# Issuing the store of a block's four sums from GpSimd in stage up 1

## The chip, the cores and the metric

One core of a Trainium2 chip. The metric is device time in microseconds, the median of several runs. Engines are named TensorE (PE in the profile; PEld are its weight loads), VectorE (DVE), ScalarE (ACT), GpSimd (POOL) and SyncE (SP). A "q" behind a name (SPq) is that engine's instruction queue.

## The reference, cut to what matters

Random-feature attention, then two feed-forward layers, all in float32:

```
x = favor_attention(q, k, v, omega)            # (2304, 512)
h = x @ w_in;   x = (h * sigmoid(h)) @ w_out   # 512 -> 2048 -> 512: up 1, down 1
g = x @ w_gate; v = x @ w_val                  # 512 -> 1536: up 2
out = (silu(g) * v) @ w_out2                   # 1536 -> 512: down 2
```

The weights of the feed-forward layers come to the kernel as 64-bit floats.

## The kernel before, in words

The program is one stream per engine, written out in advance. Its stages follow one another: attention, up 1, down 1, up 2, down 2. Each product of up and down is split into seven half-size products (a Strassen-like scheme), so a weight block is needed not only as its four quarters A11, A12, A21, A22 but also in four sums S1 to S4. Operands are split into a high and a low part, and each product is three matmuls.

**Converting a weight block** (`conv_job`, L339 on). Two loads bring the raw 64-bit words of the halves (L344). ScalarE takes the upper word (`first`, L368), VectorE shifts it (L375) and merges the lower word (`low`, L382), after which the raw slot is free again. Then GpSimd makes S1 to S4 (`sums`, L401) into one buffer of 1024 columns, which in up 1 exists once (`f_sum`). What follows depends on the block:

- a block of `w_in` is used in up 1 itself: it is split into high and low parts (`hi`, L433 on VectorE and L435 on ScalarE; `lo`, L448), and the buffer of sums is free after the last split;
- a block of moe_w_out (`down_job`) or the first block of gate and val (`up_job_dram`) is needed later: three stores put it into DRAM (L465): A22 (128 KB), A11 and A12 (256 KB), and the four sums (512 KB). The buffer of sums is free when the last has landed.

During attention three blocks of each kind are converted (there the list `early` is worked off). In up 1 the stream `conv` does the rest: blocks 3 to 7 of `w_in` and of moe_w_out by turns, then gate and val (`conv1`, at the end of the function).

**Up 1** (`up_phase(0, ...)`). For each of 24 steps seven products run on TensorE (L1133). ScalarE copies a partial result from one PSUM bank to the next or to SBUF (L1150), VectorE adds another (L1207), ScalarE applies SiLU (L1174), and SyncE stores the result (L1159).

**What sets the order.** A planner in the kernel's own Python keeps a clock per engine (`clk`), a price per kind of operation (`cost`, `dma_cost`) and a due time per result (`T`). Before each product `flush` writes out, in order of planned time, what the streams have ready. Of each stream and engine only the first entry may be placed (of the `conv` stream's ScalarE list the first two). An operation on a list can't pass the one ahead of it, and on the chip each engine works through its instructions in the order written. A DMA is an operation of its issuing engine: the planner books 0.35 us of SyncE for its issue, then a start, a duration by size and a lag, after which it counts as landed. All loads and stores of up 1 are issued by SyncE.

Of the kernel before, what the change touches and what calls it, by code (L numbers as in the profile page):

```python
# [11 lines left out]
U32 = mybir.dt.uint32  # L12
# [30 lines left out]
def kernel(  # L43
# [13 lines left out]
    nc = tc.nc  # L57
    ctx.enter_context(tc.manual_schedule())
    P = 128
# [3 lines left out]
    S = 576  # L63
# [16 lines left out]
    FP = (w_in.shape[0], w_gate.shape[0])  # L80
    wsrc = {"in": w_in, "out": w_out, "gate": w_gate, "val": w_val, "out2": w_out2}
    wsrc = {k: w.bitcast(U32) for k, w in wsrc.items()}
# [6 lines left out]
    wd_d = {k: tc.dram_tile([7, P, FP[m] * 256], F32, name=f"wd_{k}") for m, k in enumerate(DNK)}  # L89
    wu_d = {k: tc.dram_tile([P, 7 * 256], F32, name=f"wu_{k}") for k in UPK[1]}  # L90
# [12 lines left out]
    def cut(t, o, n):  # L103
        return t[:, o : o + n]
# [39 lines left out]
    clk = {e: 0.0 for e in ("PE", "ACT", "DVE", "POOL", "SP", "dma", "slot", "landed")}  # L144
# [3 lines left out]
    def cost(kind, n):  # L148
        a, b = fixed[kind]
        return a + b * n  # L150

    class Op:
        __slots__ = ("eng", "cost", "fn", "ins", "outs", "guard", "then", "slots", "live", "lead")

# [20 lines left out]
        def emit(self):  # L175
            t = max(clk[self.eng], self.ready())
            clk["slot"] = 0.0
            if self.eng == "SP":
                took, lag = self.cost
                clk["SP"] = t + 0.35  # L180
                clk["dma"] = max(t + 1.55, clk["dma"]) + took
                clk["end"] = clk["landed"] = clk["dma"] + lag
            else:
                clk["end"] = t + self.cost
            self.fn()
            if self.eng == "SP":
                end = clk["landed"]
            else:
                clk[self.eng] = end = t + self.cost
            for k in self.outs:  # L190
                T[k] = end
            if self.then is not None:
                self.then(end)
# [3 lines left out]
    def dma_cost(nbytes, kind="rows"):  # L197
        a, b = RATE[kind]
        return nbytes * a, b
# [125 lines left out]
    f_raw = Free("raw", [cut(fa, R_AT + i * 1024, 1024) for i in range(2)])  # L325
# [8 lines left out]

    halved = []

    def conv_job(kind, i, dram=None, side=False):
        b = {}
        key = lambda *k: (kind, i, *k)  # L339

        def load(h):
            def go():
                b["r", h] = r = f_raw.take()
                nc.sync.dma_start(out=r.bitcast(U32), in_=wsrc[kind][i, h])  # L344

            def then(end):

                if kind != "out2":
                    T[key("r", h)] = end + (1 if kind in ("in", "out") else 2.5)
                else:  # L350
                    T[key("r", h)] = end + 6.0

            return Op("SP", dma_cost(P * 4096, "words"), go, outs=[key("r", h)], slots=(f_raw, 1), then=then)

        def word(h, w):
            return b["r", h].bitcast(U32).rearrange("p (c w) -> p c w", w=2)[:, :, w]
# [32 lines left out]
        def blk(n):  # L389
            if n in ("A21", "A22"):  # L390
                return cut(b["c", 0], 0 if n == "A21" else 256, 256)
            if n in ("A11", "A12"):
                return cut(b["c", 1], 0 if n == "A11" else 256, 256)
            return cut(b["S"], 256 * (int(n[1]) - 1), 256)

        def sums(n, l, r, ins):
            def go():
                if n == 1:
                    b["S"] = f_sum.take()
                f = nc.gpsimd.tensor_add if n == 1 else nc.gpsimd.tensor_sub  # L400
                f(blk(f"S{n}"), blk(l), blk(r))  # L401

            return Op(
                "POOL", cost("POOL", 256), go, ins=[key(*k) for k in ins], outs=[key("S", n)],
                slots=(f_sum, 1) if n == 1 else None,
            )


        parts = ((0, 1), (1, 3), (3, 5), (5, 7))
        after = ([("f", 0)], [("f", 1)], [("S", 1), ("S", 2)], [("S", 3), ("S", 4)])  # L410

        def src(k):
            if k == 0:
                return blk("A22")
            return b["c", 1] if k == 1 else cut(b["S"], 512 * (k - 2), 512)

        def done(t):
            f_c.give(b["c", 0], t)
            f_c.give(b["c", 1], t)
            f_sum.give(b["S"], t)  # L420
# [34 lines left out]
            eng = "POOL" if side else "DVE"  # L455
            return Op(eng, cost(eng, n), go, ins=[key("hi", k)], outs=outs)

        def store(a, z, src, ins):

            b["stores"] = 3  # L460

            def go():
                o = dram(a, z)
                t = src()
                nc.sync.dma_start(out=o, in_=t.rearrange("p (o c) -> p o c", c=256) if len(o.shape) == 3 else t)  # L465
                b["stores"] -= 1
                if not b["stores"]:
                    done(clk["landed"])

            return Op("SP", dma_cost(P * (z - a) * 1024, "parts"), go, ins=[key(*x) for x in ins], outs=[key("d", a)])  # L470

        half = [load(0), load(1), first(0), first(1), shift(0), low(0), shift(1), low(1)]
        if dram is not None:
            return [
                *half,
                sums(1, "A21", "A22", [("f", 0)]),
                sums(3, "A11", "A21", [("f", 0), ("f", 1)]),
                store(0, 1, lambda: blk("A22"), [("f", 0)]),
                store(1, 3, lambda: b["c", 1], [("f", 1)]),
                sums(2, "S1", "A11", [("f", 1)]),  # L480
                sums(4, "A12", "S2", [("f", 1)]),
                store(3, 7, lambda: b["S"], [("S", n) for n in range(1, 5)]),
            ]
        f0, f1 = ("f", 0), ("f", 1)
        return [
# [25 lines left out]
    def weave(*jobs):  # L511

        ops = [*jobs[0][:8]]
        for n, j in enumerate(jobs):
            new = deque(jobs[n + 1][:8] if n + 1 < len(jobs) else ())
            for _ in range(min(2, len(new))):
                ops.append(new.popleft())
            for i, o in enumerate(j[8:]):
                ops.append(o)
                if i % 2 and new:  # L520
                    ops.append(new.popleft())
            ops += new
        return ops

    def down_job(m, i):
        k = DNK[m]
        return conv_job(
            k, i, dram=lambda a, z: wd_d[k][a:z, :, i * 256 : (i + 1) * 256].rearrange("o p c -> p o c")
        )

    def up_job_dram(k):
        return conv_job(k, 0, dram=lambda a, z: wu_d[k][:, a * 256 : z * 256])

    early = {"conv": deque(), "x": deque()}

# [184 lines left out]
    def u_of(u, b):  # L720
        return u // UB, UB * (u % UB) + b
# [185 lines left out]
    def store(u):  # L907
        B, p = u_of(u, 0)
        for b in range(UB):
            T["xd", B, p + b] = 0.0  # L910
            made["xd", B, p + b] = (step_of[0], 3, "out")
        nc.sync.dma_start(
            out=x_d[B][p : p + UB].rearrange("b p s -> p b s"), in_=xts.pop(u).rearrange("p (b s) -> p b s", b=UB)
        )
# [5 lines left out]
    for t in spare_c:  # L920
        f_c.give(t, 0.0)
    f_sum.give(spare_sum, 0.0)
    early["conv"].extend(chain(*(conv_job("in", i, side=True) for i in range(3)), *(down_job(0, i) for i in range(3))))
    early["x"].extend(x_prep(0, 0, xr1, False, "POOL", early=True))
    def two_steps(d):
# [78 lines left out]
    first_up = conv_job("in", 3)  # L1004
    for x in first_up[:2]:
        x.emit()
    for f, some in ((f_c, spare_c), (f_sum, [spare_sum])):
        n = len(f.q)
# [588 lines left out]
        lambda: x_prep(0, 2, xr2, False, "DVE", before=1, then=xr2_end),  # L1597
    ]

    rest = deque(down_job(0, i) for i in range(3, FP[0]))  # L1600
    jobs = []
    for i in range(3, FP[0]):
        jobs += [conv_job("in", i) if i > 3 else first_up, rest.popleft()]
    jobs += rest
    jobs += [up_job_dram("gate"), up_job_dram("val")]
    conv1 = [x for x in weave(*jobs) if not any(x is y for y in first_up[:2])]
    opened = []
    extra_c, extra_raw = cut(fa, XR_AT, 512), cut(fa, XR_AT + 512, 1024)
# [108 lines left out]
    jobs = []  # L1717
    for i in range(1, FP[1]):
        jobs += [conv_job("gate", i), conv_job("val", i), down_job(1, i - 1)]
# [75 lines left out]
```

## Time and profile before

| | us |
|---|---|
| median of three runs | 827.8 (827.64 to 830.42) |
| the profiled execution | 828.38 |
| its span, first to last instruction | 826.6 |
| TensorE busy in it | 814.5 |
| VectorE, ScalarE, GpSimd busy | 615.1, 558.5, 162.4 |

The profile is of one execution. A row of a timeline gives start, duration, engine, source line, operation, output and input; in brackets stands how long the engine was idle before it and what ended that. Up 1 runs from about 118 to 290 us of the span, down 1 to about 482, up 2 to about 692. TensorE has its full clock in all of it.

### The profile page before, as it was taken

To read this page: it belongs to the slowest core of one execution; us is meant where nothing else is said; L and a number is where in the kernel's file an instruction comes from. 1 tells how busy PE (TensorE), PEld (TensorE's weight loads), DVE (VectorE), ACT (ScalarE), POOL (GpSimd) and SP (SyncE) were. 2 spreads that over 40 slices of the span, in tenths; PEclk is the share of its full clock that TensorE was granted. 3 is DMA by queue.
4 is the path that set the end of the run, shared out by engine and by line. 5 is a ranking of instruction groups with operands and counts; after the bars stand their busy time and mean duration, and the time that the engine had idled before them with its cause. 6 is when DMAs were issued, how large, how long until landed. Compare 5 with 4: busy or idle time off the path is not lost.

```text
span 826.6 us, 18058 instructions
## 1 busy us (share of the span) xinstructions
PE 814.5 (99%) x6889; PEld 794.8 (96%) x6889; DVE 615.1 (74%) x982; ACT 558.5 (68%) x1172; POOL 162.4 (20%) x204
## 2 busy tenths in 40 slices
PE   8999999999999999999999999999999999999998
PEld 7878889999999999999999999999999999999998
DVE  4888877657744598995989987675656559998872
ACT  6989978867767776455577776665656558655552
POOL 0477851033442000000000113130303020000000
PEclk9999999999999999999999999999999999999999
DMA  8679956679889996538366836463636278764502
GB/s 281 197 249 277 315 186 218 201 223 328 288 266 374 395 306 213 170 115 267 116 212 230 271 102 211 126 213 105 212 107 216 101 235 318 250 217 140 164 3 77
DMA packets 112134, 175.58 MB, mean 212 GB/s; under 512 B 9648, under 2 KB 94256, under 8 KB 112048
## 3 DMA queue, kind: packets, MB, share of 16 engines
q1 hardware_dynamic: 111824, 174.20, 63.7%
q8 instruction: 54, 0.88, 0.4%
q10 hardware_dynamic: 224, 0.23, 0.1%
q14 instruction: 32, 0.26, 0.1%
HBM read 109.38 MB, written 65.01 MB: 211 GB/s over the span
## 4 chain that ended last, share of the span: by engine, by line
PE 81%; issue 6%; ACT 4%; DMA 4%; DVE 2%; POOL 1%; SPq 1%; ACTq 0%; DVEq 0%; POOLq 0%
PE ps L1133 36%; PE ps L1556 35%; PE ps L777 3%; ACT kq L793 2%; PE ps L821 2%; PE ps L837 2%; PE ps L868 2%; DMA fa<-in_moe_w_out 1%; POOL fa L401 1%; DMA g_d<-fa 1%; DMA ra<-wd_out 1%; PE ps L893 1%; DMA rawq<-in_q 1%; DVE fa L382 1%; ACT qp L839 1%
## 5 line engine op out<-in xcount | busy, mean ns | idle before, releaser
L401 POOL TENSOR_TENSOR fa<-fa 128x256 f32<-128x256 f32 x124 | 103.4, 848 | 496.2 <-DMA x_d<-fa 202.9
L1133 PE MATMUL ps<-ra 128*128 128x384 f32 x840 | 143.0, 327 | 2.2 <-ACT ps L1150 2.2
L1133 PE MATMUL ps<-rb,ra 128*128 128x384 f32 x840 | 142.4, 327 | 0.8 <-ACT ps L1150 0.8
L1133 PE MATMUL ps<-rc,ra 128*128 128x384 f32 x840 | 141.1, 326 | 0.0
L1133 PEld LDWEIGHTS ps<-ra 128*128 128x128 f32 x840 | 137.1, 189 | 3.5 <-ACT ps L1150 3.5
L1133 PEld LDWEIGHTS ps<-rb,ra 128*128 128x128 f32 x840 | 137.2, 189 | 2.0 <-ACT ps L1150 1.9
L1133 PEld LDWEIGHTS ps<-rc,ra 128*128 128x128 f32 x840 | 137.2, 189 | 0.0
L1150 ACT ACTIVATE ps<-ps 128x384 f32<-128x384 f32 x180 | 85.8, 478 | 67.2 <-PE ps L1133 58.1
L1367 ACT ACTIVATE ra<-fa 128x768 fp32r<-128x768 f32 x81 | 68.0, 843 | 64.2 <-PE ps L1556 55.1
L1556 PE MATMUL ps<-ra,rb 128*128 128x384 f32 x576 | 96.5, 326 | 0.0
L1556 PEld LDWEIGHTS ps<-ra,rb 128*128 128x128 f32 x576 | 94.1, 189 | 0.0
L1371 DVE TENSOR_TENSOR ra<-fa,ra 128x768 fp32r<-128x768 f32 x80 | 76.2, 954 | 19.6 <-ACT ra L1367 18.9
L793 ACT ACTIVATE kq<-ps,nb 128x128 f32<-128x128 f32 x288 | 79.4, 408 | 6.2 <-DVE nb L791 6.1
L1207 DVE TENSOR_TENSOR fa<-fa,ps 128x384 f32<-128x384 f32 x78 | 43.0, 552 | 35.7 <-ACT ps L1150 26.2
L1556 PE MATMUL ps<-ra 128*128 128x384 f32 x414 | 69.2, 326 | 0.0
L1556 PE MATMUL ps<-ra,rc 128*128 128x384 f32 x402 | 68.8, 326 | 0.0
L1556 PEld LDWEIGHTS ps<-ra 128*128 128x128 f32 x414 | 67.6, 189 | 0.0
L1556 PEld LDWEIGHTS ps<-ra,rc 128*128 128x128 f32 x402 | 65.9, 189 | 0.0
L1391 DVE TENSOR_TENSOR fa<-ra,fa 128x768 f32<-128x768 f32 x63 | 60.1, 954 | 0.9 <-DMA ra<-g_d 0.4
L382 DVE SCALAR_TENSOR_TENSOR fa<-fa 128x512 uint32<-128x512 uint32 x65 | 58.7, 903 | 0.7
L368 ACT ACTIVATE fa<-fa 128x512 f32<-128x512 f32 x65 | 54.3, 838 | 4.4 <-DMA fa<-in_moe_w_out 2.7
L791 DVE TENSOR_REDUCE nb<-ps 128x4 f32<-128x512 f32 x72 | 48.4, 682 | 6.3 <-PE ps L777 3.2
(128 smaller groups left out, 1153.2 us busy)
## 6 DMA issues: line engine op xcount, KB each, us to landing
g_d<-fa SPq DMA_DIRECT2D x110, 192.0 KB, 3.8
fa<-g_d SPq DMA_DIRECT2D x42, 384.0 KB, 4.6
ra<-g_d SPq DMA_DIRECT2D x42, 384.0 KB, 4.0
fa<-in_moe_w_out SPq DMA_DIRECT2D x28, 512.0 KB, 5.2
g_d<-mf SPq DMA_DIRECT2D x58, 192.0 KB, 3.9
fa<-in_moe_w_in SPq DMA_DIRECT2D x16, 512.0 KB, 5.2
wd_out<-fa SPq DMA_DIRECT2D x12, 512.0 KB, 3.3
fa<-in_moe_w_gate SPq DMA_DIRECT2D x12, 512.0 KB, 4.1
```

Of the source, the lines that this page charges most:

```text
L368: nc.scalar.activation(c, word(h, 1).bitcast(F32), AF.Prelu, scale=2.0**-112, alpha=-(2.0**32))
L382: nc.vector.scalar_tensor_tensor(c, word(h, 0), 29, c, op0=ALU.logical_shift_right, op1=ALU.bitwise_or)
L401: f(blk(f"S{n}"), blk(l), blk(r))
L791: nc.vector.reduce_max(nb, x, axis=AX.X, negate=True)
L793: nc.scalar.activation(e[:, g // 2, g % 2, h * M : (h + 1) * M], x[:, g, :], AF.Exp, bias=nb[:, g : g + 1])
L1133: nc.tensor.matmul(woven(ps[b][:, :N]), cut(l, j * P, P), halves(cut(r, j * N, N)), start=start and c == 0, stop=stop and c == 5, skip_gro ...
L1150: nc.scalar.activation(out() if callable(out) else out, src, AF.Copy)
L1207: nc.vector.tensor_add(t, t if in_place else p5[n], ps[bank_][:, :N])
L1367: nc.scalar.activation(ops[s, p, k][0], src(), AF.Copy)
L1371: nc.vector.tensor_sub(l, src(), h.bitcast(F32))
L1391: (nc.gpsimd if eng == "POOL" else nc.vector).tensor_sub(z(PLACE[to]), z(PLACE.get(l, l)), z(PLACE.get(r, r)))
L1556: nc.tensor.matmul(woven(ps[BANKS[p] + e][:, :N]), cut(a, e * P, P), halves(b), start=p in FIRST and i == 0 and c == 0, stop=p in LAST and ...
```

## The change

The store of the four sums gets an engine of its own choice: with "S" in the new argument `own` it is an operation of GpSimd, issued with `nc.gpsimd.dma_start`, in the list of GpSimd behind the sums. The planner books 1.0 us of GpSimd for the issue, and the same start, duration and lag as for SyncE. The blocks of up 1 get `own="S"`; those of attention and of up 2 keep the default. The same argument could move loads ("L"), which no block asks for.

```
+    ISSUE = {"SP": 0.35, "POOL": 1.0}
...
-            if self.eng == "SP":
+            if isinstance(self.cost, tuple):
                 took, lag = self.cost
-                clk["SP"] = t + 0.35
+                clk[self.eng] = t + ISSUE[self.eng]
                 clk["dma"] = max(t + 1.55, clk["dma"]) + took
                 clk["end"] = clk["landed"] = clk["dma"] + lag
...
-        def store(a, z, src, ins):
+        def store(a, z, src, ins, eng="SP"):
...
-                nc.sync.dma_start(out=o, in_=t.rearrange("p (o c) -> p o c", c=256) if len(o.shape) == 3 else t)
+                by = nc.gpsimd if eng == "POOL" else nc.sync
+                by.dma_start(out=o, in_=t.rearrange("p (o c) -> p o c", c=256) if len(o.shape) == 3 else t)
...
-            return Op("SP", dma_cost(P * (z - a) * 1024, "parts"), go, ins=[key(*x) for x in ins], outs=[key("d", a)])
+            return Op(eng, dma_cost(P * (z - a) * 1024, "parts"), go, ins=[key(*x) for x in ins], outs=[key("d", a)])
...
-                store(3, 7, lambda: b["S"], [("S", n) for n in range(1, 5)]),
+                store(3, 7, lambda: b["S"], [("S", n) for n in range(1, 5)], "POOL" if "S" in own else "SP"),
...
-    rest = deque(down_job(0, i) for i in range(3, FP[0]))
+    OWN = "S"
+    rest = deque(down_job(0, i, OWN) for i in range(3, FP[0]))
...
-    jobs += [up_job_dram("gate"), up_job_dram("val")]
+    jobs += [up_job_dram("gate", OWN), up_job_dram("val", OWN)]
```

## Rows read from the trace of the kernel before

**Rows 1.** The page, part 1: busy us, share of the span, instructions.
```profile
PE 814.5 (99%) x6889; PEld 794.8 (96%) x6889; DVE 615.1 (74%) x982; ACT 558.5 (68%) x1172; POOL 162.4 (20%) x204
```

**Rows 2.** Windows: start:end, us, busy us (instructions) by engine, clock, DMA share, GB/s.
```profile
118.00:290.00 172.00, 169.49 (x1072) 166.91 (x1072) 110.83 (x196) 129.22 (x268) 42.88 (x48) 1.00 0.85 289
482.00:692.00 210.00, 210.00 (x1294) 210.00 (x1294) 136.16 (x234) 130.25 (x263) 47.96 (x60) 1.00 0.53 177
692.00:827.00 135.00, 131.06 (x807) 130.76 (x805) 103.38 (x124) 73.85 (x112) 0.00 (x0) 1.00 0.46 152
```

**Rows 3.** Waits of the weight loads, 115 to 292 us; then their timeline.
```profile
PEld ps L1133 <- ACT ps L1150: 4.7, 8, 1.5
...
190.35 0.95 PEld L1133 LDWEIGHTS ps<-ra 128*128 128x128 f32 x6 [0.53 <-ACT ps L1150]
...
195.01 0.95 PEld L1133 LDWEIGHTS ps<-rb,ra 128*128 128x128 f32 x6 [0.79 <-ACT ps L1150]
...
233.52 0.95 PEld L1133 LDWEIGHTS ps<-ra 128*128 128x128 f32 x6 [1.48 <-ACT ps L1150]
235.04 10.70 PEld L1133 LDWEIGHTS ps<-ra 128*128 128x128 f32 x66 [0.58 <-ACT ps L1150]
```

**Rows 4.** SyncE's queue: its waits, 170 to 262 us; then its timeline.
```profile
SPq L465 <- POOL fa L401: 12.3, 6, 3.2
...
179.31 0.50 SPq L344 DMA_DIRECT2D fa<-in_moe_w_out  x1
181.44 0.45 SPq L344 DMA_DIRECT2D fa<-in_moe_w_in  x1
...
222.00 3.94 SPq L465 DMA_DIRECT2D wd_out<-fa  x2
225.99 0.50 SPq L344 DMA_DIRECT2D fa<-in_moe_w_out  x1
```

**Rows 5.** Timeline of GpSimd in up 1.
```profile
182.23 2.93 POOL L401 TENSOR_TENSOR fa<-fa 128x256 f32<-128x256 f32 x4 [3.37 <-DMA wd_out<-fa]
196.80 2.93 POOL L401 TENSOR_TENSOR fa<-fa 128x256 f32<-128x256 f32 x4 [3.39 <-DMA wd_out<-fa]
212.43 2.92 POOL L401 TENSOR_TENSOR fa<-fa 128x256 f32<-128x256 f32 x4 [3.40 <-DMA wd_out<-fa]
220.74 4.80 POOL L401 TENSOR_TENSOR fa<-fa 128x256 f32<-128x256 f32 x4 [5.39 <-DVE ra L448]
229.64 2.91 POOL L401 TENSOR_TENSOR fa<-fa 128x256 f32<-128x256 f32 x4 [4.10 <-DMA wd_out<-fa]
```

**Rows 6.** Timeline of VectorE in up 1.
```profile
174.50 0.76 DVE L382 SCALAR_TENSOR_TENSOR fa<-fa 128x512 uint32<-128x512 uint32 x1
...
191.66 1.19 DVE L382 SCALAR_TENSOR_TENSOR fa<-fa 128x512 uint32<-128x512 uint32 x1
...
221.18 0.79 DVE L382 SCALAR_TENSOR_TENSOR fa<-fa 128x512 uint32<-128x512 uint32 x1
```

**Rows 7.** Timeline of ScalarE in up 1.
```profile
185.87 0.62 ACT L435 ACTIVATE ra<-fa 128x512 fp32r<-128x512 f32 x1
...
189.06 0.86 ACT L368 ACTIVATE fa<-fa 128x512 f32<-128x512 f32 x1 [0.65 <-DMA fa<-in_moe_w_in]
...
193.34 0.53 ACT L1174 ACTIVATE fa<-fa 128x384 f32<-128x384 f32 x1 [1.18 <-DVE fa L1207]
...
201.10 0.61 ACT L435 ACTIVATE ra<-fa 128x512 fp32r<-128x512 f32 x1
...
216.61 0.62 ACT L435 ACTIVATE ra<-fa 128x512 fp32r<-128x512 f32 x1
...
232.42 0.66 ACT L368 ACTIVATE fa<-fa 128x512 f32<-128x512 f32 x1 [2.49 <-DMA fa<-in_moe_w_out]
...
236.79 0.61 ACT L435 ACTIVATE ra<-fa 128x512 fp32r<-128x512 f32 x1
```

**Rows 8.** All transfers that write or read wd_out: issue to landing.
```profile
DMA to landing us min/median/max: 1.9/5.0/7.9
```

More of the change, by code (lines that the diff above doesn't have):

```diff
@@ L185, in emit @@
             self.fn()
-            if self.eng == "SP":
+            if isinstance(self.cost, tuple):
                 end = clk["landed"]
@@ L335, with conv_job @@
     halved = []
-    def conv_job(kind, i, dram=None, side=False):
+    def conv_job(kind, i, dram=None, side=False, own=""):
         b = {}
@@ L343, in go @@
                 b["r", h] = r = f_raw.take()
-                nc.sync.dma_start(out=r.bitcast(U32), in_=wsrc[kind][i, h])
+                (nc.gpsimd if "L" in own else nc.sync).dma_start(out=r.bitcast(U32), in_=wsrc[kind][i, h])
             def then(end):
@@ L351, in then @@
                     T[key("r", h)] = end + 6.0
-            return Op("SP", dma_cost(P * 4096, "words"), go, outs=[key("r", h)], slots=(f_raw, 1), then=then)
+            return Op("POOL" if "L" in own else "SP", dma_cost(P * 4096, "words"), go, outs=[key("r", h)], slots=(f_raw, 1), then=then)
         def word(h, w):
@@ L523, in weave, with down_job, up_job_dram @@
         return ops
-    def down_job(m, i):
+    def down_job(m, i, own=""):
         k = DNK[m]
         return conv_job(
-            k, i, dram=lambda a, z: wd_d[k][a:z, :, i * 256 : (i + 1) * 256].rearrange("o p c -> p o c")
+            k, i, dram=lambda a, z: wd_d[k][a:z, :, i * 256 : (i + 1) * 256].rearrange("o p c -> p o c"), own=own
         )
-    def up_job_dram(k):
-        return conv_job(k, 0, dram=lambda a, z: wu_d[k][:, a * 256 : z * 256])
+    def up_job_dram(k, own=""):
+        return conv_job(k, 0, dram=lambda a, z: wu_d[k][:, a * 256 : z * 256], own=own)
     early = {"conv": deque(), "x": deque()}
@@ L1598 @@
     ]
-    rest = deque(down_job(0, i) for i in range(3, FP[0]))
+    OWN = "S"
+    rest = deque(down_job(0, i, OWN) for i in range(3, FP[0]))
     jobs = []
     for i in range(3, FP[0]):
-        jobs += [conv_job("in", i) if i > 3 else first_up, rest.popleft()]
+        jobs += [conv_job("in", i, own=OWN) if i > 3 else first_up, rest.popleft()]
     jobs += rest
-    jobs += [up_job_dram("gate"), up_job_dram("val")]
+    jobs += [up_job_dram("gate", OWN), up_job_dram("val", OWN)]
     conv1 = [x for x in weave(*jobs) if not any(x is y for y in first_up[:2])]
```

## The prediction

> **What bounds the kernel now.** I read the page's table of engines first: TensorE has work for 99% of the span [rows 1]. Then the stages, each as one window: up 1 has 169.49 us of matmul in 172.00 us, up 2 has none to spare (210.00 in 210.00), and what is missing in down 2 (131.06 in 135.00) is mostly the end of the program [rows 2]. The change touches up 1, so its own matmul sets the limit and all that an edit can give back is what TensorE waits there. The waits of the weight loads say how much that is: 4.7 us in 8 waits, every one for a ScalarE copy of L1150 [rows 3]. Four of them carry most: 0.53 and 0.79 us near 190 and 195 us, 1.48 and 0.58 us near 233 and 235 us [rows 3].
>
> Next, why ScalarE was late with those copies. It works in order. At 232.42 it had stood 2.49 us in front of a conversion (L368) whose raw weights had not landed; the copy that TensorE wanted was behind it. At 189.06 the same with 0.65 us [rows 7]. And why had the weights not landed? SyncE's queue is in order too. The two stores that begin at 222.00 take until 225.94, because the second is the store of the four sums and stands until GpSimd has made them (220.74 + 4.80 = 225.54); the load of moe_w_out is issued at 225.99, right behind it [rows 4, 5]. The raw slot that this load fills had been free since the VectorE operation that began at 221.18 ended, at 221.97 [rows 6]. So the load stood 4 us behind a store that it has nothing to do with. The queue's waits give the sum for all of them: SyncE stood 12.3 us in 6 waits for GpSimd's sums [rows 4].
>
> **The change part by part.** Seven stores of 512 KB leave SyncE's queue: five blocks of moe_w_out (indices 3 to 7) and the single blocks of gate and val. The three blocks converted during attention don't get the new argument, and up 2's don't either. Loads stay where they are, because the argument holds no "L".
>
> *Removed from SyncE:* seven issues (about 0.4 us each, under other work and worth nothing by themselves) and the 12.3 us of standing. In the planner the store also leaves SyncE's list of the conversion stream, of which only the first entry may be placed, so the next loads are planned earlier as well as run earlier. At 222 us: the load goes at about 222.4 in place of 225.99, 3.6 us sooner. With the 6.4 us that it then took to release ScalarE (225.99 to 232.42), it has landed by 228.8; ScalarE was free for it from 229.93 (232.42 - 2.49). The wait goes, and with it 1.48 + 0.58 = 2.06 us of TensorE. At 179.31 the first load follows a store of sums in the same way, and the load of 181.44, the third in that train, is what ScalarE stood for at 189.06 [rows 4, 7]; the train starts some 3 us sooner, so this 0.53 us goes too. The 0.79 us at 195.01 I don't count: there ScalarE stood 1.18 us for VectorE, not for a load [rows 7]. Gain: 2.06 + 0.53 = 2.6 us. What is late next at those places is PE's own rate.
>
> *Added to GpSimd:* seven issues, between a block's four sums and the next block's four. No row shows a transfer issued by GpSimd, so neither the issue nor the landing has a price. GpSimd's own time costs nothing: behind the store it stands anyway until the one buffer of sums is free, 3.39 us and 4.10 us in the rows [rows 5]. What counts is by how much the next sums are later than now; call it L. Queued behind them are the next `w_in` block's sums, and ScalarE's conversion of S3 and S4 (L435, 128x512) waits for these. The slack between the last sum and that conversion, over the four blocks: 185.16 to 185.87 = 0.71; 199.73 to 201.10 = 1.37; 215.35 to 216.61 = 1.26; 232.55 to 236.79 = 4.24, of which 2.06 goes with the stall, so 2.18 [rows 5, 7]. TensorE gives another 0.4 us (2.49 us of ScalarE cost 2.06). A block thus costs nothing until L passes 1.1, 1.8, 1.7 and 2.6 us. Bounds for L: transfers of this tensor land 1.9 to 7.9 us after issue, median 5.0 [rows 8]; against the 3.4 to 4.1 us that the store of sums needs now, L lies between -2.2 and 4.5. At the low end nothing is lost. I take the median, 5.0 - 3.4 = 1.6 and 5.0 - 4.1 = 0.9, and round up to L = 1.5: the store now starts on a queue that has drained while SyncE stood, and will run beside loads issued ahead of it. That costs 1.5 - 1.1 = 0.4 us in the first block and nothing in the others.
>
> The Trainium skill names a hazard here: by "SBUF — State Buffer", section "SBUF: two separate sides", a transfer issued by GpSimd has its descriptors written by GpSimd's cores, and VectorE in a two-port mode locks them out until its instruction ends. No run here shows such a transfer yet; by the page's figures (620 ns alone, 3,100 ns beside a VectorE copy) L would be about 2.5 us, an estimate, and the change would come out even. This hazard is the mechanism of the slower rival below, where its price is worked out from rows.
>
> *VectorE beside GpSimd:* the same operation (L382) takes 0.76 and 0.79 us mostly alone and 1.19 us at 191.66, beside sums [rows 6]. A store may hold up one VectorE operation as the sums do, by 0.4 us; bounds 0 (VectorE has room in up 1) and 7 x 0.4 = 2.8 us. Nearer is the low end, since the trace shows one such delay among its waits of TensorE (at 195.01): I take 0.6.
>
> *Moved elsewhere:* SyncE's later loads of down 1 start when the conversion stream is empty; they sit 20 us ahead of need, and the last store now leaves when its sums end. I take 0, bounds ±1 us for how ScalarE's order falls there.
>
> **Sum.** -2.6 + 0.4 + 0.6 = -1.6 us, all of it in up 1. The profiled execution took 828.38 us (span 826.6 and 1.8 around it); it would be 826.8. The median of the runs, 827.8, lies 0.6 lower, and becomes 826.2.
>
> **The rivals.**
> *No change* (827.8, within 0.7): the stall moves rather than goes. The seven loads start sooner, and a store on its own queue takes bandwidth from them; ScalarE meets the next late operand instead, and 195.01 shows that VectorE stands ready to be that. Against it: at 233 us nothing else was late within 2 us. The Trainium skill speaks for this rival: "DMA: Bandwidth & Descriptors", section "Issuing engines are not separate DMA queues", says that issuing from several engines saves only issue time; by that rule the gain is seven issues under other work, and the time stays 827.8. The trace disagrees as to what that saves here, since SyncE stood 12.3 us in order, not in issue.
>
> *Slower, by late sums.* One mechanism: the store issued by GpSimd lands so late that ScalarE stands in front of S3 and S4 of the `w_in` blocks, as it does now in front of raw weights. Gain and loss cancel at L = 2.4 (1.3 + 0.6 + 0.7 + 0 = 2.6). At L = 3.5 it costs 2.4 + 1.7 + 1.8 + 0.9 = 6.8, net +4.2: 832.0. At the bound, 4.5: 3.4 + 2.7 + 2.8 + 1.9 = 10.8, net +8.2: 836.0. For it: the first block's slack is only 0.71 us, and the planner prices the landing as for SyncE. Against: the median landing leaves L at 1.5.
>
> *All stalls go:* the planner's new order happens to remove every wait of up 1; -4.3 us (4.7 less what the matmul pipe hides): 823.5. The waits after 260 us have other causes, so little speaks for it.
>
> **How the numbers follow.** About 0.5% (4.1 us) is what a measurement of this kernel tells from no change. Forecast 0.54 (its own range 824.6 to 827.2), no change 0.23, slower 0.20, all stalls 0.03. More than 0.5% faster needs nearly every stall of up 1: 0.03. More than 0.5% slower needs L above 3.5, about half of the slower case, and something for an unlucky new order: 0.13. The rest, 0.84, is within. The range 824.0 to 832.0 leaves out the last case and the far end of the third.
>
> **What would show it.** Right: no wait of SyncE for GpSimd's sums in up 1; loads of moe_w_out issued some 3 us sooner against the sums; ScalarE's 2.49 us in front of L368 gone; TensorE's waits in up 1 down from 4.7 to 2 to 3 us; down 1 starting 1 to 2 us sooner. Wrong: ScalarE waiting for GpSimd at L435, or GpSimd standing 6 us and more for its store; a row of VectorE operations stretched at the seven issues; new waits in up 2, whose order I take to be as before.

## The result, and the profile after

The change makes the kernel slower by 1.1%: 835.66 us in the median of 6 runs, against 827.72 us for the kernel before in the same comparison. The ratio is 1.0108, with a 95% interval of 1.009 to 1.0127. The forecast was 826.2 us, the range 824.0 to 832.0. What came is the rival "slower, by late sums". Of the ten times of one kernel below (two buffers, the change) one was 1710.22 us, at the full clock and for a reason that is not known; its ratio leaves that one out.

Up 1 is where it is lost. Its first product starts at 117.2 us of the span (118.4 before, with nothing changed ahead of it), and down 1's first product at 295.6 (289.6 before): up 1 takes 178.4 us in place of 171.2. After it the two executions differ by 0.5 us.

First, the wait that the change was to remove. SyncE's timeline after, at the block of [rows 4]'s line at 179.31: the loads of moe_w_out go out at 174.52, three microseconds before the sums of the block ahead are made (172.87 + 4.78 = 177.65).

```profile
174.10 0.37 SPq L468 DMA_DIRECT2D wd_out<-fa  x1
174.52 2.05 SPq L346 DMA_DIRECT2D fa<-in_moe_w_out  x2
```

SyncE no longer waits for GpSimd's sums between 170 and 262 us. Nor does ScalarE stand for raw weights to speak of: 0.6 us in one wait, where it stood 2.49 and 0.65 us [rows 7]. Of the waits of TensorE at 190, 195, 233 and 235 us [rows 3] the last three have gone with it; at 190 the same weight loads wait longer than before (191.08 below), for another reason.

Now what has come in. GpSimd's timeline after, beside [rows 5]; L468 is the store that it now issues, the bracket what it waited for:

```profile
172.87 4.78 POOL L403 TENSOR_TENSOR fa<-fa 128x256 f32<-128x256 f32 x4 [42.08 <-DVE ra L450]
177.95 1.12 POOL L468 DMA_DIRECT2D wd_out<-fa  x1 [0.31 <-POOL fa L403]
185.04 4.18 POOL L403 TENSOR_TENSOR fa<-fa 128x256 f32<-128x256 f32 x4 [5.98 <-DMA wd_out<-fa]
...
209.87 5.56 POOL L403 TENSOR_TENSOR fa<-fa 128x256 f32<-128x256 f32 x4 [3.73 <-DVE ra L450]
215.73 0.77 POOL L468 DMA_DIRECT2D wd_out<-fa  x1 [0.30 <-POOL fa L403]
222.95 3.85 POOL L403 TENSOR_TENSOR fa<-fa 128x256 f32<-128x256 f32 x4 [6.46 <-DMA wd_out<-fa]
```

The last sum of a block ends at 177.65 and the next block's first begins at 185.04: 7.4 us, where the kernel before needed 3.4. At 215.43 to 222.95 it is 7.5 us. So L, the lateness that the prediction put at 1.5 us, is 4.0. The sums themselves also ran longer: 4.18, 3.11, 3.85 and 3.43 us for the four `w_in` blocks, where the kernel before needed 2.91 to 2.93. Counted from the last sum of the block ahead, the last sum of these four blocks thus comes 5.3, 4.1, 5.1 and 3.7 us later than before. ScalarE's waits (total, times, longest) and its timeline show who pays:

```profile
ACT ra L437 <- POOL fa L403: 10.0, 3, 4.2
```

```profile
184.54 0.49 ACT L1153 ACTIVATE ps<-ps 128x384 f32<-128x384 f32 x1
189.26 0.63 ACT L437 ACTIVATE ra<-fa 128x512 fp32r<-128x512 f32 x1 [4.23 <-POOL fa L403]
189.79 0.47 ACT L1153 ACTIVATE fa<-ps 128x384 f32<-128x384 f32 x1
...
226.84 0.63 ACT L437 ACTIVATE ra<-fa 128x512 fp32r<-128x512 f32 x1 [3.84 <-POOL fa L403]
...
243.36 0.63 ACT L437 ACTIVATE ra<-fa 128x512 fp32r<-128x512 f32 x1 [1.91 <-POOL fa L403]
```

It stands in front of the conversion of S3 and S4, and the copy that TensorE needs (L1153) is written behind it. TensorE's waits over up 1, and the large ones:

```profile
PEld ps L1136 <- ACT ps L1153: 10.1, 7, 3.7
```

```profile
191.08 0.95 PEld L1136 LDWEIGHTS ps<-ra 128*128 128x128 f32 x6 [2.60 <-ACT ps L1153]
...
227.90 0.95 PEld L1136 LDWEIGHTS ps<-rc,ra 128*128 128x128 f32 x6 [3.73 <-ACT ps L1153]
...
247.88 2.90 PEld L1136 LDWEIGHTS ps<-ra 128*128 128x128 f32 x18 [2.13 <-ACT ps L1153]
```

The first two, 2.60 and 3.73 us, follow ScalarE's two long stands. The third has another cause: the copy that ends it stood behind an operation (L1177) that waited for an addition of VectorE.

```profile
246.38 0.52 ACT L1177 ACTIVATE fa<-fa 128x384 f32<-128x384 f32 x1 [1.62 <-DVE fa L1210]
...
247.36 0.47 ACT L1153 ACTIVATE ps<-ps 128x384 f32<-128x384 f32 x1
```

The same 18 weight loads wait 1.87 us in a kernel below in which ScalarE never stands for sums.

10.1 us in place of 4.7 is 5.4 of the 7.2 us. Another 1.7 is a slower clock after the first of these waits: 24 weight loads from 192.00 took 5.61 us, where 24 at the full clock take 3.93.

```profile
192.00 5.61 PEld L1136 LDWEIGHTS ps<-rb,ra 128*128 128x128 f32 x24
...
200.50 3.93 PEld L1136 LDWEIGHTS ps<-rc,ra 128*128 128x128 f32 x24
```

The windows below (PE, PEld, DVE, ACT and POOL busy with instructions, then the granted clock) give the same: a clock of 0.53 and of 0.62 for 2 us each loses 0.94 + 0.76 = 1.7 us.

```profile
190.00:192.00 2.00, 0.92 (x6) 0.92 (x6) 1.05 (x3) 2.00 (x5) 0.72 (x1) 1.00 0.52 189
192.00:194.00 2.00, 2.00 (x8) 2.00 (x8) 1.97 (x4) 1.00 (x3) 1.04 (x2) 0.53 0.15 51
194.00:196.00 2.00, 2.00 (x10) 2.00 (x9) 1.10 (x2) 1.55 (x4) 1.62 (x2) 0.62 0.98 192
196.00:198.00 2.00, 2.00 (x14) 2.00 (x13) 1.65 (x3) 0.97 (x2) 0.78 (x1) 1.00 1.06 372
```

### The profile page after: what moved, and what is told of

Same layout as the page of the kernel before. It is cut to its first block, busy times and chain, and to the rows that moved or that the text cites. A ratio compares the mean times of both kernels' runs of the same rounds, so it can differ in the third digit from the quotient of the medians.

```text
span 833.0 us, 18059 instructions
## 1 busy us (share of the span) xinstructions
PE 817.0 (98%) x6889; PEld 797.2 (96%) x6889; DVE 620.8 (75%) x982; ACT 557.3 (67%) x1172; POOL 172.1 (21%) x211
## 4 chain that ended last, share of the span: by engine, by line
PE 79%; issue 6%; DMA 5%; DVE 3%; POOL 3%; ACT 3%; SPq 1%; ACTq 0%; POOLq 0%; DVEq 0%
PE ps L1559 34%; PE ps L1136 34%; PE ps L780 4%; POOL fa L403 3%; DMA wd_out<-fa 2%; PE ps L824 2%; PE ps L840 2%; PE ps L871 2%; ACT kq L796 1%; DMA g_d<-fa 1%; DVE fa L384 1%; PE ps L896 1%; DMA rawq<-in_q 1%; DVE ra L450 0%; ACT fa L370 0%
## 5 line engine op out<-in xcount | busy, mean ns | idle before, releaser
L403 POOL TENSOR_TENSOR fa<-fa 128x256 f32<-128x256 f32 x124 | 107.2, 878 | 490.4 <-ACT fa L1177 222.5
L1136 PEld LDWEIGHTS ps<-rb,ra 128*128 128x128 f32 x840 | 138.9, 191 | 0.3 <-ACT ps L1153 0.3
L1153 ACT ACTIVATE ps<-ps 128x384 f32<-128x384 f32 x180 | 85.6, 476 | 71.0 <-PE ps L1136 64.2
L1210 DVE TENSOR_TENSOR fa<-fa,ps 128x384 f32<-128x384 f32 x76 | 41.9, 551 | 33.8 <-ACT ps L1153 24.8
L384 DVE SCALAR_TENSOR_TENSOR fa<-fa 128x512 uint32<-128x512 uint32 x65 | 61.0, 939 | 0.7
```

Of the source, the lines that this page charges most:

```text
L384: nc.vector.scalar_tensor_tensor(c, word(h, 0), 29, c, op0=ALU.logical_shift_right, op1=ALU.bitwise_or)
L1136: nc.tensor.matmul(woven(ps[b][:, :N]), cut(l, j * P, P), halves(cut(r, j * N, N)), start=start and c == 0, stop=stop and c == 5, skip_gro ...
L1153: nc.scalar.activation(out() if callable(out) else out, src, AF.Copy)
L1210: nc.vector.tensor_add(t, t if in_place else p5[n], ps[bank_][:, :N])
```

## The experiments

Two things changed at once: who issues the store, and the planner's order (the loads pass the store in its lists). And one thing had to be explained: why the store takes 7.4 us to give its buffer back. In the table, "gap" is the time from the last sum of a moe_w_out block to the next block's first where the landing ended the wait, and "stands" is ScalarE's wait for sums. Blocks are compared in up 1 unless said otherwise.

| kernel | median us | ratio to before (95%) | gap us | stands us |
|---|---|---|---|---|
| before | 827.4 to 827.9 | | 3.4 to 4.1 | 0 |
| the change | 835.66 | 1.0108 (1.009 to 1.0127) | 6.8 to 7.5 | 10.0 |
| new order, SyncE issues | 830.42 | 1.0043 (1.0025 to 1.0061) | 4.4 to 7.4 | 5.7 |
| old order, GpSimd issues | 841.0 | 1.0172 (1.0147 to 1.0196) | 6.4 to 9.2 | 14.8 |
| the change, planner told | 839.72 | 1.0143 (1.0128 to 1.0158) | 6.6 to 7.6 | 4.9 |
| gate and val only | 828.4 | 1.0009 (0.9996 to 1.0022) | | 0 |
| two buffers, the change | 828.09 | 1.0006 (0.9996 to 1.0016) | | 0 |
| two buffers, before | 827.49 | 0.9994 (0.9984 to 1.0004) | | 0 |
| two buffers, new order, SyncE | 827.06 | 0.9989 (0.998 to 0.9998) | | 0 |

**Order against issuer.** Two runs complete the square.

```
-                by = nc.gpsimd if eng == "POOL" else nc.sync
+                by = nc.sync
```

> The planner places the store exactly as in the change (in GpSimd's list, 1.0 us of GpSimd booked, loads no longer behind it), but SyncE issues it. This splits the new order from the new issuer. Theory (late sums from the slow landing of a GpSimd store): landing 3.5 to 5 us after the sums, ScalarE's waits for sums under 3 us, time 826 to 829, perhaps below before since the loads pass the store. Rival 1 (the new order costs): 833 to 836. If the landing is slow because loads are now ahead of the store on the DMA rings and not because of the issuer, the store lands 6 to 7 us after the sums here too and the time is 832 or more.

830.42 us: 2.8 us slower than before, not better. SyncE's store, now behind loads in its own queue, lands late too. The two rows are the issues of the 512 KB stores between 170 and 262 us (count, size, median us to landing), before and here:

```profile
wd_out<-fa SPq DMA_DIRECT2D x5, 512.0 KB, 3.2
```

```profile
wd_out<-fa SPq DMA_DIRECT2D x5, 512.0 KB, 6.4
```

The same engine issues the same bytes, and the landing takes twice as long once the loads go first. The third clause of the expectation said that this would cost 832 or more; the landing came, the cost was smaller.

```
-            return Op(eng, dma_cost(P * (z - a) * 1024, "parts"), go, ...)
+            return Op("SP", dma_cost(P * (z - a) * 1024, "parts"), go, ...)
```

> The order of every engine is that of the kernel before, instruction for instruction; only the seven stores move from SyncE's queue to GpSimd's. Together with before, the change and the run that kept the new order with SyncE as issuer this fills a table of order against issuer. Theory (the store lands late when loads no longer wait behind it, and the one buffer of sums then holds up the next block): the store lands 6 to 7.5 us after the sums, ScalarE waits 5 to 10 us for sums, 831 to 836. Rival (the planner's new order is the cost): 826 to 829.

841.0 us, worse than expected, with the order of TensorE, ScalarE and VectorE unchanged to the instruction. So to move the store to GpSimd costs 13 us in the old order and 5 us in the new one (835.66 - 830.42); the new order softens it, and costs 3 us where SyncE issues. The new order as the main cost is ruled out. Not all of the 13 us is waiting: in the profile of the old order, stretches at a lower clock cost 3.3 us (66 weight loads in three groups took 14.10 us in place of some 10.8).

**No w_in block behind.**

```
-    rest = deque(down_job(0, i, OWN) for i in range(3, FP[0]))
+    rest = deque(down_job(0, i) for i in range(3, FP[0]))
```

> Only the stores of gate and val are issued by GpSimd; no w_in block follows either, so no sums that ScalarE needs can be late. The five moe_w_out stores are SyncE's again. Theory (late sums): within 1.5 us of before, 826.5 to 829, SyncE's waits for sums back to 10 us and more, no wait of ScalarE for GpSimd. Rival 2 (each such store costs by itself, through VectorE): two sevenths of 8 us, 830. Rival 1 (packed order): 827 to 828, as the theory.

828.4 us: no difference that can be told. A store issued by GpSimd costs nothing where no needed sums wait for its buffer, though GpSimd waits 6.8 us for gate's. That is no sign of a slow issuer: in the kernel before, where SyncE issues gate's store among other transfers, it waits as long.

```profile
257.00 3.52 POOL L401 TENSOR_TENSOR fa<-fa 128x256 f32<-128x256 f32 x4 [7.30 <-DMA wu_gate<-fa]
```

A cost per store through VectorE would have shown as 2 us.

**A second buffer of sums.** Three result slots of 384 columns are given up for it and come back after up 1.

```
-        "sum": [],
+        "sum": [cut(more_f, 0, 1024)],
...
-        "s": [cut(more_f, 0, 384), ..., cut(more_f, 1536, 384)],
+        "s": [cut(more_f, 1152, 384), cut(more_f, 1536, 384)],
```

> The change with a second buffer for the sums in up 1 (1024 columns taken from three of the fifteen result slots of 384), so that the next w_in block's sums need not wait for the store to land. Theory (late sums): ScalarE's waits for sums gone, SyncE's wait for sums gone as well, so the 2.6 us of gain shows: 824 to 828, if three fewer result slots cost nothing. Rival 1 and rival 2: 833 or more, since order and issuer stay.

828.09 us: all 8 us of loss are gone, with GpSimd still the issuer and the loads still early. This shows that the whole loss comes from the late sums, the time at the slower clock included: the clock is full in all of up 1 here. The gain of 2.6 us did not come, though. Two controls say where it is:

> The kernel before with the second buffer of sums, the control for the change with two buffers (828.1). SyncE still issues and still stands for the sums. Theory (the second buffer alone frees the chain, the issuer then has little to give): 826 to 828.5, SyncE's waits for sums still 8 us or more. If the issuer's gain was hidden in that run under the cost of three fewer result slots, this one takes 830 or more.

> Two buffers of sums and the new order, with SyncE as issuer: the loads pass the store in the order, and no sums wait for its landing. Theory (with the second buffer the landing doesn't matter, so neither does the issuer): within 1.5 us of the change with two buffers, 826.5 to 829.5. Rival (GpSimd's issue itself holds up VectorE's additions, on which ScalarE stood 12.6 us in that run): 2 us or more faster than it, 826 or less, with these waits down by a third.

827.49 and 827.06 us. The second buffer by itself gives nothing that can be told, and with it the issuer matters by 1.0 us at most (828.09 against 827.06). The last is the fastest kernel of this study, by 0.1%. In it TensorE waits 3.3 us in up 1 (4.7 before), 1.87 of them at 240.17, at the loads that wait at 247.88 in the change. The rows are TensorE's wait, then the timelines of ScalarE and VectorE ahead of it:

```profile
240.17 2.90 PEld L1136 LDWEIGHTS ps<-ra 128*128 128x128 f32 x18 [1.87 <-ACT ps L1153]
```

```profile
238.66 0.52 ACT L1177 ACTIVATE fa<-fa 128x384 f32<-128x384 f32 x1 [2.42 <-DVE fa L1210]
```

```profile
234.96 0.79 DVE L384 SCALAR_TENSOR_TENSOR fa<-fa 128x512 uint32<-128x512 uint32 x1
235.69 0.39 DVE L435 CAST ra<-fa 128x512 fp32r<-128x512 f32 x1
236.01 0.95 DVE L377 TENSOR_SCALAR fa<-fa 128x512 uint32<-128x512 uint32 x1
236.88 1.28 DVE L450 TENSOR_TENSOR ra<-fa,ra 128x512 fp32r<-128x512 f32 x2
238.09 0.54 DVE L1210 TENSOR_TENSOR fa<-fa,ps 128x384 f32<-128x384 f32 x1
```

Weights that come sooner are converted sooner, and the addition (L1210) that ScalarE needs stands behind a row of conversions. Part of the gain turned into this wait; the kernel before has none at these loads. Planning the conversions less, or further, ahead didn't remove it:

```
-        "conv": Stream(1.5, ACT=2),
+        "conv": Stream(1.0, ACT=2),
```

> Two buffers of sums and SyncE as issuer in the new order (827.1), with the conversion stream planned only 1.0 us ahead of TensorE instead of 1.5. In that run the longest wait of TensorE (1.87 us at 240) was an addition of VectorE behind a row of conversions placed ahead of it. Theory (that is where the rest of the gain went): the wait shrinks below 1 us and the time is 825 to 827. Rival (the weights of the last blocks are due as they are made, so that placing them later only moves the wait): 827 to 830.

833.3 us (1.0073, 1.0061 to 1.0086): TensorE now waits 3.17 us for a low part of weights (L450) at 240, and 2.44 us for ScalarE at 245. The weights of the last `w_in` blocks are due nearly as they are made.

> Two buffers of sums and SyncE as issuer in the new order (827.1), with the conversion stream planned 2.0 us ahead of TensorE instead of 1.5 (1.0 gave 833.3, with a wait for the weights of a late block). If the due weights set the limit, conversions placed earlier take away the wait at 240: 825 to 827. If VectorE's burst ahead of the additions sets it, the wait grows: 828 to 832.

827.92 us (1.0004, 0.9992 to 1.0015): neither of the two answers. The waits at 240 shrink to 1.02, and 1.48 us appear at 254.6.

**Can the planner hide it?** It had priced the landing as SyncE's.

```
-                clk["end"] = clk["landed"] = clk["dma"] + lag
+                clk["end"] = clk["landed"] = clk["dma"] + lag + (3.7 if self.eng == "POOL" else 0.0)
```

> The change as it is, but the planner is told that a store issued by GpSimd lands 3.7 us later than one of SyncE (about what the trace of the change shows). Theory (the sums of the next w_in block come 4 us later than planned, and ScalarE, written in the planned order, stands 10.0 us in three waits for them): the conversions of S3 and S4 are written later, these waits fall below 2 us in all, TensorE's waits in up 1 fall from 10.1 to 3 to 5 us, time 827 to 830. Rival 1 (the new order itself, loads packed closer, is what costs): no better than 833. Rival 2 (GpSimd's descriptor writing holds up VectorE): no better than 833.

839.72 us, so that expectation failed. ScalarE stands less (4.9 us), but TensorE now waits for the weights themselves, 11.1 us in all:

```profile
PEld ps L1136 <- DVE ra L450: 6.5, 2, 4.7
PEld ps L1136 <- ACT ps L1153: 4.6, 4, 1.9
```

All blocks pass through one buffer of sums, a `w_in` block and a stored block by turns. Each late landing pushes the chain back, and by the last blocks the weights themselves are late. So this plan does not hide the landing; whether another could is open. Nor are the 4.1 us by which it is slower than the change all waiting: the waits of TensorE are 1.0 us more, and the slower clock costs 1.4 us more. It was 0.50 to 0.57 from 244 to 254 us, and 40 weight loads there, in three groups, took 9.58 us in place of some 6.5; that is 3.1 us, against 1.7 in the change. The middle group:

```profile
249.53 1.78 PEld L1136 LDWEIGHTS ps<-ra 128*128 128x128 f32 x6 [1.77 <-ACT ps L1153]
```

**Why the store lands late.** The same store in up 2, six times:

```
-        jobs += [conv_job("gate", i), conv_job("val", i), down_job(1, i - 1)]
+        jobs += [conv_job("gate", i), conv_job("val", i), down_job(1, i - 1, "S")]
```

> Up 1 as before; the six stores of sums of up 2's moe_w_out blocks are issued by GpSimd instead, in a stage with about half of the DMA engines' time taken (0.53 against 0.85 in up 1). It prices the landing. Theory A (the store is slow because other transfers share the DMA engines): the next sums start 3.5 to 5 us after the store's sums. Theory B (a transfer issued by GpSimd is slow by itself): 6 us and more here too. Time: within 2 us of before by A, 2 to 8 us more by B.

828.46 us (1.0005, 0.9996 to 1.0015). GpSimd's timeline, a block in the middle and the last:

```profile
581.49 0.77 POOL L468 DMA_DIRECT2D wd_out<-fa  x1 [0.30 <-POOL fa L403]
589.24 3.79 POOL L403 TENSOR_TENSOR fa<-fa 128x256 f32<-128x256 f32 x4 [6.98 <-DMA wd_out<-fa]
...
663.50 0.77 POOL L468 DMA_DIRECT2D wd_out<-fa  x1 [0.41 <-POOL fa L403]
667.26 0.72 POOL L403 TENSOR_TENSOR fa<-fa 128x256 f32<-128x256 f32 x1 [2.99 <-DMA wd_out<-fa]
```

Five of the six have sums behind them, and neither theory holds for all five. Where the next block's loads are under way the wait is 6.98 us; at the last block, with no loads left, it is 2.99, and the gap is 4.2 us (3.1 with SyncE as issuer). Two runs with the old order and GpSimd as issuer test that in up 1. In the first, SyncE again stands for the sums, by a small store of its own:

```
...
+                if eng == "POOL":
+                    nc.sync.dma_start(out=tiny_d, in_=cut(t, 960, 64))
...
```

> The kernel with the old order and GpSimd as issuer (841.0), and in SyncE's queue, at the old place of each of the seven stores, a small store (64 columns of S4, 32 KB, to a scratch of its own) that has to wait for the sums. So SyncE stands as before, and the loads again come behind the sums; GpSimd still issues the 512 KB. Theory (of the 4 us by which the store lands later, about 3 are the loads that now run beside it, 1 is the issuer's): the next sums start 4 to 6 us after the last ones instead of 7 to 8.5, ScalarE's waits for sums fall from 14.8 to below 8 us, time 829 to 835. Rival (GpSimd's transfer is slow by itself): 7 us and more, 839 or more.

842.63 us (1.0184, 1.0169 to 1.02), no better, and the gap stays at 6.7 to 7.4 us in four of five blocks. By itself this speaks for the rival. But the loads were not behind the store: SyncE's and GpSimd's timelines show the load issued at 179.21, 0.4 us after the sums, when GpSimd had not finished its own issue (179.12 + 1.13):

```profile
178.84 0.32 SPq L471 DMA_DIRECT2D tiny_d<-fa  x1
179.21 0.42 SPq L347 DMA_DIRECT2D fa<-in_moe_w_out  x1
```

```profile
179.12 1.13 POOL L469 DMA_DIRECT2D wd_out<-fa  x1 [0.31 <-POOL fa L404]
186.23 3.60 POOL L404 TENSOR_TENSOR fa<-fa 128x256 f32<-128x256 f32 x4 [5.98 <-DMA wd_out<-fa]
```

In the second, SyncE's small transfer reads what GpSimd has stored, so that SyncE issues nothing, neither loads nor stores, until that has landed:

```
...
+                if eng == "POOL":
+                    nc.sync.dma_start(out=tiny_d, in_=o[:, 3, :64] if len(o.shape) == 3 else cut(o, 960, 64))
...
```

> As the run with the small store, but SyncE's small transfer reads the last columns of what GpSimd has just stored, so SyncE stands until the 512 KB have landed and no load is issued beside them. It prices the landing in up 1 without the loads. Theory (the loads beside it make the store slow): the next sums start 4 to 5.3 us after the last ones, ScalarE's waits for sums fall below 6 us; the loads come 4 to 5 us later than in the kernel before, so ScalarE stands for raw weights instead and the time stays above 833. Rival (GpSimd's transfer is slow by itself): 6.5 us and more after the last sums, as with the loads beside it.

850.01 us (1.0272, 1.0254 to 1.0289), and the gap is 3.8 to 4.2 us in four of five blocks, 5.1 in one:

```profile
173.47 4.82 POOL L404 TENSOR_TENSOR fa<-fa 128x256 f32<-128x256 f32 x4 [42.09 <-DVE ra L451]
178.60 1.10 POOL L469 DMA_DIRECT2D wd_out<-fa  x1 [0.31 <-POOL fa L404]
182.44 2.91 POOL L404 TENSOR_TENSOR fa<-fa 128x256 f32<-128x256 f32 x4 [2.73 <-DMA wd_out<-fa]
```

This settles it. Alone, a store issued by GpSimd gives its buffer back 0.4 to 0.8 us later than one of SyncE in four of five blocks (3.8 to 4.2 against 3.4; at the last block of up 2 it is 1.1 us later). The rest of L, 3.2 to 3.6 us, comes from what SyncE issues beside it, loads of 512 KB above all: in up 2, beside the store at 540.55, SyncE issued two loads and nothing else until 547.43, and GpSimd waited 6.80 us. The time is worse because the loads now come late: ScalarE stands 14.1 us for raw weights of moe_w_out, TensorE waits 22.3 us in up 1, and its clock falls to 0.50 twice (from 246 and from 280 us).

## Why the prediction was wrong, by its own steps

*What bounds the kernel, and what the change removes:* right. SyncE's waits for sums went, the loads left three to four microseconds sooner, and ScalarE's long stand for raw weights went with the waits of TensorE at 233 and 235 us. The one at 190 lost this cause and got a worse one.

*The gain of 2.6 us:* too large by itself. With the loss taken away by a second buffer, what is left is 0.1%, 0.8 us (827.06 against 827.86), and the next thing late is VectorE at 240. "At 233 us nothing else was late within 2 us" did not hold once the conversions had moved.

*L = 1.5 us:* this is the step that failed. "I take the median, 5.0 - 3.4 = 1.6 and 5.0 - 4.1 = 0.9, and round up" used the median landing of all transfers of wd_out: loads and stores of 128 to 512 KB, with all kinds of neighbours. Measured: 4.0. With L = 4.0 the prediction's formula gives 2.9 + 2.2 + 2.3 + 1.4 = 8.8 for its four blocks, less 2.6 is +6.2, or 834.0 in the terms of its median; 835.66 came. That this is near is in part luck. The second block cost nothing (its conversion was written later, and began at 206.88, after the last sum at 206.13), the third cost 3.73 us of TensorE in place of 2.3, and the formula knows neither the longer sums nor the 1.7 us at the slower clock. The bounds held L (-2.2 to 4.5) and the range did not hold the time, because half of the slower case was cut from it. The prediction even named the cause, that the store starts "on a queue that has drained while SyncE stood, and will run beside loads issued ahead of it", and gave it next to nothing. The 3.4 us were the landing of a store that was first in a drained queue (in the trace before, the DMA engines' busy share was 0.00 from 178.5 to 179.5 us, around its issue at 178.89, and the loads came behind it), and the wait that was to be removed is what gave it that. Removing the wait takes both sides: the loads go first, and the store pays.

*The planner:* priced in the rival as "the planner prices the landing as for SyncE". Telling it the true landing did not help (839.72), and a second buffer did (828.09): what was late was the one buffer, and writing the conversions later did not make it less late.

*The hazard of the Trainium skill:* "SBUF — State Buffer", section "SBUF: two separate sides", would have descriptors of a GpSimd transfer starved by VectorE. No run here shows a delay of that size: alone, the store is 0.4 to 0.8 us later than SyncE's with VectorE at work beside its issue (in the last run above, L385 from 217.37 to 218.16 beside the issue from 217.35 to 218.12, and the next sums 3.8 us behind the last). Whether these are operations of the kind that the Trainium skill means there, no run shows. So the slower rival came, but by another mechanism than the one that the prediction took from there. The other page of the Trainium skill, "DMA: Bandwidth & Descriptors", section "Issuing engines are not separate DMA queues", says that transfers of all issuers run on the same 16 DMA engines and interleave. The trace agrees (3.4 us to landing alone, 6.9 beside the loads), and that was the warning: the prediction read the rule for what the change might save, and not for what the store would lose by no longer being first.

*VectorE beside GpSimd, 0.6 us:* small, as taken. Between 170 and 262 us VectorE's merges (L382 before, L384 after) grew from 932 to 1054 ns in the mean of 22, 2.7 us of VectorE in all. That is near the upper bound of 2.8 for VectorE, but what it costs TensorE is 1.0 us at most, the difference that the issuer makes with two buffers; the change on gate and val alone cost nothing that can be told. *Up 2 in the same order:* one new wait of 0.44 us. *Not foreseen:* the longer sums, and the 1.7 us at the slower clock.

## What to carry to other kernels

A queue that stands for a semaphore also holds back what would compete with the transfer at its head; before such a wait is taken away, ask what will then be on the DMA engines beside that transfer, and who waits for it to land. Take the price of a landing from rows with the same neighbours, not from a median over all of them. And a buffer that exists once ties the stages on both sides of it together: here a second one left 1.0 us at most of the issuer's 5 to 13.

## What the runs showed of the hardware

- A transfer of 512 KB issued by GpSimd holds GpSimd for 0.77 to 1.13 us (0.57 to 0.75 us where its rows are 4 KB and not 1 KB long), after 0.3 to 0.4 us in which it waits for its own last sum; SyncE's issue takes about 0.4 us.
- Issue to landing, 512 KB, GpSimd: 3.4 us alone and 6.9 us beside loads (medians of five each). SyncE: 3.2 us ahead of the loads, 6.4 us behind them.
- After a wait of TensorE of 2.60 us the granted clock was 0.53 and 0.62 over the 4 us from 192; within them it was 0.50, the lower of its two levels, from 193 to 195 us. After one of 3.73 us, 37 us later, it stayed at 1.00 (228 to 230 us). With the new order and SyncE as issuer it was 0.50 from 244 to 247 us, after waits of 1.63 and 1.40 us. So the length of the last wait does not tell whether the clock falls; what does stays open.
- The stretches at the lower clock belong to the loss: 1.7 us in the change, about 3 us in each of two kernels above, none in the kernels of 829 us and less.
